# Attention and a split-precision feed-forward layer in one kernel: the low part of the inner layer given to ScalarE and GpSimd beside the last attention units, and room made for their keys

## The chip, the core and the metric

The kernel runs on one core of one Trainium2 chip. The metric is the device time of one execution in microseconds (us). Five engines work side by side, each through its own queue in order: TensorE (PE; PEld is its weight load), VectorE (DVE), ScalarE (ACT), GpSimd (POOL) and SyncE (SP), which issues most transfers.

## What is computed

```python
# q_l, k_l, v_l: 8 batches x 8 heads x 512 x 64;  q_g, k_g, v_g: 8 x 8 x 32 x 64
k_all, v_all = concat(k_g, k_l), concat(v_g, v_l)
out_g = softmax(q_g @ k_all.T / 8) @ v_all            # 32 global queries see all 544 keys
s_l   = concat(q_l @ k_g.T / 8, where(|i-j| <= 32, q_l @ k_l.T / 8, -1e9))
out_l = softmax(s_l) @ concat(v_g, v_l)               # 512 local queries: a band and the globals
x  = concat(out_g, out_l) as (8, 576, 512)
xn = (x - mean) / sqrt(var + 1e-6) * g_ln             # over the last axis
out = x + relu(xn @ w_ch1) @ w_ch2                    # 512 -> 2048 -> 512
```

## The kernel before

**Units and chunks.** Attention is done in units. 64 local units (a batch, a pair of heads, a half of 256 queries) come first; then 8 global units, each of four batches and a pair of heads (128 rows, 544 keys). Rows that are done make chunks for the feed-forward layer: chunks 0 to 7 of 512 local rows, and chunk 8 of the 256 global rows. While TensorE runs the layer for one chunk, the attention of the next is fitted in between.

**The layer** (class `Ffn`). A product in float32 quality is made of three products of high and low parts. For each of 16 inner blocks f, `first` makes 12 matmuls of 512 columns (line 836) into the bank `ph`; ScalarE writes the high part `hh` = relu(ph) (line 845); VectorE writes the low part `hl` = max(ph, 0) - hh (line 849). `second(f-1, t)`, four groups of 3 matmuls (line 861), takes `hh` and `hl` of the block before. So TensorE's order is first(f), second(f-1), first(f+1), second(f), and there is one `ph` for chunks of 512 rows.

**Visits.** At a visit TensorE computes the scores of one global unit (lines 667 and 678) and, right behind them, the weighted sums of the unit before (line 745). Between two visits VectorE takes row minima from the scores (`lowest`, line 690), ScalarE the exponentials (line 701), and the weights are turned: by VectorE in 16 or 32 transposes of 32x128 (line 729) into `gpt`, and partly by TensorE (`turn`, line 715) with a ScalarE copy (line 719), as `BY_DVE` says for each unit. The last 32 keys' weights go by four transposes (`turn_last`, line 736) onto the diagonal of a zeroed tile `lasts`, and meet a stacked tail of the values, `gvt` (64 KB).

**Transfers.** A unit's queries (`gq`, 128 KB, two buffers), keys (`gk`, 1152 KB, one buffer) and values (`tmp`, 1024 KB in two transfers, and `gvt`) are loaded by SyncE's queue. After a visit that scores unit n come n's values, then the queries and keys of n+1. The tiles of the global units lie in the pool `apool1`, which takes the place of the local units' pool `apool0` (u_e, u_v, p, pt).

**Order.** Each engine's queue is written out ahead by a planner (`Plan.emit`). Every operation has an engine, a cost, a key and what it must follow; of what can start soonest, the smallest key goes first. The table `ORDER` fixes each queue up to the middle of chunk 5; from there the costs decide. For the transfers the planner reckons 0.9 per loading step of a global unit, sizes of 1.2 (keys) and 1.15 (values) MB at `WIRE` = 0.42 MB per us, and a visit's cost as

```python
cost = 0.42 + 0.55 * len(us) + 1.12 * len(prev) + (0.1 if us and prev else 0)
```

`LATENCY` is 0.2 and `LANDING` 0.5. Chunk 7 may hold visits from the places `GLOBAL` = (0, 4, 8, 11, 14, 17, 20, 24) on, in half blocks of the layer; a visit whose inputs the planner sees later comes later. The chip itself waits for the real data, by semaphores.

Of the kernel before, what the change touches and what calls it, by code (L numbers as in the profile page):

```python
# [54 lines left out]
LAST_SUMS = 17  # L55
SOONER = 6.0
SECOND = 20.0
FIRST = 22
BEHIND = 2.1
GAP = 2.2  # L60
# [19 lines left out]
APPLY_ACT = (1,)  # L80
IN_FLIGHT = 8
STORING = 6.0
BY_DVE = (4, 4, 4, 0, 0, 0, 0, 0)

ORDER = {
    "PE": """
# [220 lines left out]
class Operation:  # L307
    def __init__(self, engine, cost, key, run, after, behind, late, size):
        self.engine, self.cost, self.key, self.run = engine, cost, key, run
        self.after = flat(after)  # L310
        self.behind, self.late, self.size, self.end = behind, late, size, None

    def lands(self):
        return self.end + self.late + LATENCY

    def ready(self):
        t = self.behind.end if self.behind else 0.0
        for a in self.after:
            same = a.engine == self.engine and not a.size
            t = max(t, a.end if same else a.end + a.late + LATENCY)  # L320
        return t

@with_exitstack
def attention_ffn_kernel(
# [1 line left out]
    tc: tile.TileContext,  # L326
    eq: bass.AP,
    ev: bass.AP,
    gq: bass.AP,
    gk: bass.AP,  # L330
    gv: bass.AP,
    gt: bass.AP,
# [6 lines left out]
    NQ, NV = eq.shape[4], ev.shape[4]  # L339
    D = P // 2  # L340
    SG = WIN
    SA = gk.shape[4] - SG
    S = SA - SG
    DM = HP * P
    KT = DM // P
# [15 lines left out]
    def f32(ap):  # L361
        return ap.bitcast(F32)
# [153 lines left out]
    class Local:  # L516
# [7 lines left out]
        def load(self, part):  # L524

            if self.alone:
                if part != 1:
                    shape, tag = [P, 2 * (KT * P + DM)], UNITS[units.index(self)]
                    u = wpool.tile(shape, F32, name="u", tag=tag)
                    self.parts = u[:, :NQ], u[:, NQ:NQ + NV]  # L530
            elif part == 0:
                self.parts = self.ap.tile([P, NQ], F32, name="u_e", bufs=2), None
            else:
                self.parts = self.parts[0], self.ap.tile([P, NV], F32, name="u_v", bufs=2)
            self.e, v = self.parts
            if v is not None:
                self.v = v.rearrange("p (w d) -> p w d", w=8)
            dma(self.parts[part], (eq, ev)[part][self.at])

        def score(self, sc):  # L540
            self.mn = small.tile([P, 4], F32, name="mn", bufs=4)
            self.sm = small.tile([P, 4], F32, name="sm", bufs=4)
            self.p = self.ap.tile([P, 4, P], F32, name="p", bufs=3)
            self.sc = sc
            for qb in range(2):
                for g in range(4):
                    gp = slice(g * WIN, (g + 1) * WIN)
                    w = 4 * qb + g
                    k0 = 8 + w + w // 3
                    for h in range(2):  # L550
                        hd = slice(h * D, (h + 1) * D)
                        nc.tensor.matmul(  # L552
                            sc[h][gp, qb * P:(qb + 1) * P],
                            self.e[hd, w * WIN:(w + 1) * WIN],
                            self.e[hd, k0 * WIN:(k0 + 4) * WIN],
                            start=True,
                            stop=True,
                            tile_position=(h * D, g * WIN),
                            skip_group_check=True,
                        )  # L560
# [77 lines left out]
    class Global:  # L638
# [4 lines left out]
        def load(self, part):  # L643
            ap = self.ap
            if part == 0:
                self.q = ap.tile([P, BG, 2 * SG], F32, name="gq", bufs=2)
                self.k = ap.tile([P, BG, SA + SG], F32, name="gk")
                dma(self.q, gq[self.at])
                dma(self.k, gk[self.at])
            else:  # L650
                self.v = [wtmp.tile([P, 2, 4, P], F32, name="tmp", bufs=2) for _ in range(BG // 2)]
                self.t = ap.tile([P, P], F32, name="gvt")
                for k, v in enumerate(self.v):
                    dma(v, gv[self.at][:, 2 * k:2 * k + 2])
                dma(self.t, gt[self.at])
# [75 lines left out]
        def turn_last(self):  # L731


            for i in range(BG):
                ip = slice(i * SG, (i + 1) * SG)
                nc.vector.transpose(out=lasts[0][ip, :, ip], in_=self.p[ip, :, 512:SA])

        def sums(self, pv):
            self.pv = pv
            for h in range(2):  # L740
                hd = slice(h * D, (h + 1) * D)
                for c in range(5):
                    for i in range(BG):
                        ip = slice(i * SG, (i + 1) * SG)
                        nc.tensor.matmul(  # L745
                            pv[ip, hd],
                            self.pt[:, h, c, ip] if c < 4 else lasts[0][:, h, ip],
                            self.v[i // 2][:, i % 2, c, hd] if c < 4 else self.t[:, hd],
                            start=c == 0,
                            stop=c == 4,  # L750
                            tile_position=(0, i * SG),
                            skip_group_check=True,
                        )
# [66 lines left out]
    class Ffn:  # L820
# [20 lines left out]
        def high(self, f):  # L841
# [2 lines left out]
            self.hq[f] = hh, hl  # L844
            nc.scalar.activation(hh[:, :self.n], self.ph[f][:, :self.n], AF.Relu)  # L845

        def low(self, f):
            hh, hl = self.hq[f]
            nc.vector.scalar_tensor_tensor(  # L849
                hl[:, :self.n], self.ph[f][:, :self.n], 0.0, f32(hh[:, :self.n]),  # L850
                ALU.max, ALU.subtract,
            )
# [55 lines left out]
    pools = []  # L908

    def begin(phase):  # L910
        if pools:
            pools.pop().__exit__(None, None, None)
        if phase == 2:
            wcm.__exit__(None, None, None)
            return
        cm, ap = open_pool(f"apool{phase}")
        pools.append(cm)
        for u in phases[phase]:
            u.ap = ap
        if phase == 1:  # L920
            last = ap.tile([P, 2, P], F32, name="lasts")
            nc.gpsimd.memset(last, 0.0)
            lasts.append(last)

    lasts = []

    def into(u):

# [7 lines left out]
    def begin_plan(plan):  # L936
# [229 lines left out]
        def visit(key, us, prev, nxt):  # L1166
# [31 lines left out]
            for j, u in enumerate(us):  # L1198
                exps = []
                before = []  # L1200
                if locals_:
                    for k in range(4):
                        before.append(op("DVE", 0.21, key + 0.1, lambda u=u, k=k: u.lowest(k), v,
                                         before[-1:], late=0.1))
                        exps.append(op("ACT", 0.39, key + 0.2, lambda u=u, k=k: u.exp(k), before[-1],
                                       late=0.1))
                        banks[k // 2].append(before[-1])
                else:
                    for h in range(2):
                        for part in range(2):  # L1210
                            before.append(op("DVE", (0.65, 0.15)[part], key + 0.1,
                                             lambda u=u, h=h, part=part: u.lowest(h, part), v,
                                             before[-1:], late=0.1))
                            banks[2 if part else h].append(before[-1])
                        exps.append(op("ACT", 0.75, key + 0.2, lambda u=u, h=h: u.exp(h), before[-1],
                                       late=0.2))
                t = op("POOL", 0.23, key + 0.3, lambda u=u: u.total(), exps)
                inverse_of[u] = op("DVE", 0.17, key + 1.0, lambda u=u: u.inverse(), t)
                if not locals_:
                    u.parts = n = BY_DVE[phases[1].index(u)]  # L1220
                    rr, o = [], []
                    for k in range(32 if n else 16):
                        o.append(
                            op("DVE", 0.31 if k < 16 else 0.06 + 0.25 * n / 4, key + (2 if k < 16 else SECOND),
                               lambda u=u, k=k: u.transposes(k // 16, k // 4 % 4, k % 4),
                               exps[k // 16], o[-1:])
                        )
                    last = op("DVE", 0.5, key + 2, lambda u=u: u.turn_last(), exps, o[0])
                    if n < 4:
                        t = op("PE", 0.1 + 0.45 * (4 - n) / 4, key + 1.0, lambda u=u: u.turn(att(1, "tp")), use(1, rr),  # L1230
                               exps[1], late=0.3)
# [87 lines left out]
        pe = [None]  # L1319
        turns_free = flat(list(low.values()))  # L1320
        hh, hl, second, adds, outs = {}, {}, {}, {}, {}
        xts = {0: (xt, (xh, xl))}

        def chain(*args, **kw):
# [3 lines left out]
        for c, chunk in enumerate(chunks):  # L1328
# [29 lines left out]
            for f in range(NF + 1):  # L1358
                key = nominal(c, f)
                if f < NF:  # L1360
                    for i, k in enumerate((2, 1, 0)):
# [5 lines left out]
                        waits = []  # L1367
                        if i == 0:
                            if not wide:
                                waits = [hl.get((c, f - 2)), hl[c - 1, NF - 1] if f == 0 else None,  # L1370
                                         use(0, []) if f == 1 else None]
                            else:
                                waits = [hl.get((c, f - 1)) if f else hl.get((c - 1, NF - 1))]
                            if c == f == 0:
                                waits += lowest[n0 - 2] + lowest[n0 - 1]
                        if f == 1 and i == 0 and 0 in beside:
# [10 lines left out]
                    if 2 * f in beside:  # L1387
                        beside[2 * f].behind = end
                    hh[c, f] = op("ACT", 0.59 if wide else 0.38, key - URGENT, lambda f=f, box=box: box[0].high(f),
                                  end, second.get((c, f - 2, nt - 1)))  # L1390
                    hl[c, f] = op("DVE", 0.66 if wide else 0.39, key - URGENT, lambda f=f, box=box: box[0].low(f),
                                  hh[c, f])
                if f:
                    for t in range(nt):
                        waits = []
# [179 lines left out]
```

## Time and profile before

| | |
|---|---|
| median of 3 runs | 903.01 us (901.91 to 903.97) |
| profiled execution | 904.45 us |
| its span, first to last instruction | 902.3 us |
| TensorE busy | 886.8 us (98%) |
| VectorE busy | 724.1 us (80%) |
| ScalarE busy | 309.7 us (34%) |
| GpSimd busy | 40.7 us (5%) |
| moved by transfers | 119.87 MB |

An engine's busy time is a share of the whole span, and matmuls overlap, so "busy" for TensorE means that it has no gap, not that each matmul runs at its shortest. The idle time ahead of an instruction names what ended it.

### The profile page before, as it was taken

The page shows a single profiled execution, that of the slowest core. Times are in us where ns is not written, and L with a number is a line of the kernel's source. Part 1 is how long each engine was busy: PE and PEld are TensorE (multiplying, and loading weights), DVE is VectorE, ACT ScalarE, POOL GpSimd, SP SyncE. Part 2 cuts the span into 40 slices and gives each one's busy share as a digit, 9 for nine tenths or more (in the row PEclk, how much of TensorE's full clock was granted, in tenths as well). Part 3 has the DMA queues.
Part 4 walks back from the last instruction along what each step waited for, and adds up shares of the span by engine and source line. Part 5 has one row for each costly group of instructions (what it writes and reads, how often), then busy time and mean ns, then how long its engine had stood idle before and what let it go on. Part 6 is the DMA issues. An engine that isn't in the chain of part 4 may idle for free.

```text
span 902.3 us, 21499 instructions
## 1 busy us (share of the span) xinstructions
PE 886.8 (98%) x8493; PEld 704.9 (78%) x8493; DVE 724.1 (80%) x2544; ACT 309.7 (34%) x878; POOL 40.7 (5%) x133
## 2 busy tenths in 40 slices
PE   7899999999999999999999999999999999999998
PEld 4588787777787787878788787778778777777897
DVE  5899999789878888788878897888879998866611
ACT  7798873232224222322323222322323222222211
POOL 4100100000000000000000000000000000000000
PEclk9899999999999999999999999999999999999999
DMA  9697736324034313324332403332331524455400
GB/s 347 246 330 219 282 110 208 103 79 149 34 111 140 117 52 126 102 78 149 107 100 99 149 2 123 106 119 103 125 102 48 187 94 151 174 183 178 138 22 23
DMA packets 44021, 119.87 MB, mean 133 GB/s; under 512 B 5265, under 2 KB 7313, under 8 KB 42897
## 3 DMA queue, kind: packets, MB, share of 16 engines
q1 hardware_dynamic: 43728, 118.25, 38.0%
q8 instruction: 66, 1.08, 0.5%
q14 instruction: 35, 0.28, 0.1%
q10 hardware_dynamic: 192, 0.26, 0.1%
HBM read 100.67 MB, written 17.83 MB: 131 GB/s over the span
## 4 chain that ended last, share of the span: by engine, by line
PE 81%; DVE 2%; DMA 2%; SPq 0%; issue 0%
PE ph L836 37%; PE acc L861 37%; PE sc L552 3%; PE pv L607 3%; DMA gk<-in_gk 2%; PE pv L745 1%; PE sc L667 1%; DVE pt L599 1%; DVE xl L814 0%; DVE ob L873 0%; DVE w L466 0%; SPq L411 0%; DVE hl L849 0%; PE tp L715 0%; DVE tmp L456 0%
## 5 line engine op out<-in xcount | busy, mean ns | idle before, releaser
L861 PE MATMUL acc<-w,hh 128*128 128x512 f32 x1088 | 342.1, 395 | 0.0
L836 PE MATMUL ph<-xh,w 128*128 128x512 f32 (+1 forms) x1216 | 307.9, 379 | 0.8 <-DVE hl L849 0.6
L836 PEld LDWEIGHTS ph<-xh,w 128*128 128x128 f32 x1216 | 215.5, 188 | 49.0 <-DVE hl L849 1.1
L861 PEld LDWEIGHTS acc<-w,hh 128*128 128x128 f32 x1088 | 204.8, 188 | 47.9
L845 ACT ACTIVATE hh<-ph 128x512 fp32r<-128x512 f32 (+1 forms) x144 | 82.9, 576 | 440.1 <-PE ph L836 410.5
L861 PE MATMUL acc<-w,hl 128*128 128x512 f32 x544 | 217.9, 401 | 0.0
L599 DVE STREAM_TRANSPOSE pt<-p 32x128 f32<-32x128 f32 x768 | 207.2, 289 | 8.5
L849 DVE SCALAR_TENSOR_TENSOR hl<-ph,hh 128x512 fp32r<-128x512 f32 (+1 forms) x144 | 95.3, 662 | 101.4 <-ACT hh L845 100.4
L836 PE MATMUL ph<-xl,w 128*128 128x512 f32 x512 | 141.2, 397 | 0.0
L576 ACT ACTIVATE p<-p,mn 128x128 f32<-128x128 f32 x256 | 99.7, 392 | 93.3 <-DVE mn L564 93.2
L804 DVE STREAM_TRANSPOSE tmp<-x 32x128 f32<-32x128 f32 x384 | 116.1, 302 | 5.8
L861 PEld LDWEIGHTS acc<-w,hl 128*128 128x128 f32 x544 | 102.1, 188 | 23.8
L836 PEld LDWEIGHTS ph<-xl,w 128*128 128x128 f32 x512 | 95.6, 188 | 23.7 <-DVE xl L814 0.2
L564 DVE CUSTOM_DVE_ANT_0 p<-sc,mask 128x128 f32<-128x128 f32 x256 | 60.9, 285 | 21.7 <-PE sc L552 21.2
L729 DVE STREAM_TRANSPOSE gpt<-gp 32x128 f32<-32x128 f32 x176 | 53.3, 303 | 2.9
L576 ACT ACTIVATION_READ_ACCUMULATOR p<-p,mn 128x1 f32 x256 | 48.2, 188 | 0.0
L619 POOL TENSOR_SCALAR ri<-sm 128x4 f32<-128x4 f32 x64 | 16.9, 264 | 640.3 <-ACT p L576 638.6
L626 DVE TENSOR_TENSOR x<-pv,ri 128x256 f32<-128x256 f32 x64 | 24.8, 418 | 11.1 <-PE pv L607 11.1
L552 PEld LDWEIGHTS sc<-u_e 64*32 64x32 f32 x1792 | 24.9, 105 | 10.2 <-issue 8.8
L552 PE MATMUL sc<-u_e 64*32 64x128 f32 x1792 | 32.4, 274 | 0.0
L607 PE MATMUL pv<-u_v,pt 128*32 128x64 f32 x1792 | 30.8, 220 | 0.0
L607 PEld LDWEIGHTS pv<-u_v,pt 128*32 128x32 f32 x1792 | 26.3, 110 | 5.7 <-issue 5.7
(71 smaller groups left out, 493.4 us busy)
## 6 DMA issues: line engine op xcount, KB each, us to landing
u_v<-in_ev SPq DMA_DIRECT2D x56, 512.0 KB, 4.8
u_e<-in_eq SPq DMA_DIRECT2D x56, 336.0 KB, 5.9
raw<-in_wd SPq DMA_DIRECT2D x32, 512.0 KB, 7.1
gk<-in_gk SPq DMA_DIRECT2D x8, 1152.0 KB, 7.6
xs<-x SPq DMA_DIRECT2D x32, 256.0 KB, 6.3
ob<-xs SPq DMA_DIRECT2D x32, 256.0 KB, 5.3
out<-ob SPq DMA_DIRECT2D x32, 256.0 KB, 3.4
tmp<-in_gv SPq DMA_DIRECT2D x16, 512.0 KB, 4.7
```

The costliest lines, as they stand in the source:

```text
L552: nc.tensor.matmul(sc[h][gp, qb * P:(qb + 1) * P], self.e[hd, w * WIN:(w + 1) * WIN], self.e[hd, k0 * WIN:(k0 + 4) * WIN], start=True, sto ...
L564: nc.vector.tensor_tensor_reduce(out=self.p[:, c], in0=self.sc[h][:, qb * P:(qb + 1) * P], in1=masks[self.at[2], qb], scale=-QSCALE, scala ...
L576: nc.scalar.activation(self.p[:, c], self.p[:, c], AF.Exp, bias=self.mn[:, c:c + 1], scale=-1.0, accum_out=self.sm[:, c:c + 1],)
L599: nc.vector.transpose(out=self.pt[rp, :, gp], in_=self.p[gp, :, rp])
L607: nc.tensor.matmul(pv[gp, qb * P + h * D:qb * P + h * D + D], self.pt[:, 2 * h + qb, gp], self.v[:, 4 * qb + g, h * D:(h + 1) * D], start= ...
L626: nc.vector.tensor_tensor(self.x[:, :, hp * P:(hp + 1) * P].rearrange("p q (h d) -> p q h d", h=2), self.pv[:, :256].rearrange("p (q h d) ...
L729: nc.vector.transpose(out=self.pt[rp, h, :n, ip], in_=p[ip, :, r])
L804: nc.vector.transpose(out=dst[rp, 2 * half:2 * half + 2, :, i], in_=src[ip, :, k:k + 2, r])
L836: nc.tensor.matmul(self.ph[f][:, :self.n], w[:, kt, :], xx[kt][:, :self.n], start=begins and kt == 0, stop=ends and kt == KT - 1,)
L845: nc.scalar.activation(hh[:, :self.n], self.ph[f][:, :self.n], AF.Relu)
L849: nc.vector.scalar_tensor_tensor(hl[:, :self.n], self.ph[f][:, :self.n], 0.0, f32(hh[:, :self.n]), ALU.max, ALU.subtract,)
L861: nc.tensor.matmul(self.acc[t], a[:, ts], w, start=(f == 0 and i == 0), stop=(f == NF - 1 and i == 2),)
```

## The change

Four things are changed. From block 11 of chunk 6 to block 14 of chunk 7, except each chunk's last block, the low part is made in two steps: ScalarE writes relu(ph) a second time as plain float32 (`hw`), and GpSimd subtracts `hh` from it (`low_pool`); `ph` is free after ScalarE's second write. Units 3 and 4 are turned wholly by VectorE (`BY_DVE`). Queries and keys of a unit come in one transfer into one tile, in a pool of its own (`bp`) that takes the place of the local units' u_e and p; all else is in `ap`. The last keys' weights are turned by one transpose of all 128 rows into a tile `gl`, and the tail of the values has zeros in the other batches' rows instead (256 KB). Besides, some costs in the planner are altered: VectorE's transposes and minima are a little dearer, the last keys' cheaper, and the minima may follow a visit's scores 1.2 sooner (`SUMS`) where sums stand behind the scores.

```diff
+SUMS = 1.2
+LOW_ON_POOL = {6: 22, 7: 0}
-BY_DVE = (4, 4, 4, 0, 0, 0, 0, 0)
+BY_DVE = (4, 4, 4, 4, 4, 0, 0, 0)
...
-            t = max(t, a.end if same else a.end + a.late + LATENCY)
+            t = max(t, a.end if same else a.end + a.late + LATENCY - (SUMS if a is self.scored else 0.0))
...
-                self.parts = self.ap.tile([P, NQ], F32, name="u_e", bufs=2), None
+                self.parts = self.bp.tile([P, NQ], F32, name="u_e", bufs=2), None
...
-            self.p = self.ap.tile([P, 4, P], F32, name="p", bufs=3)
+            self.p = self.bp.tile([P, 4, P], F32, name="p", bufs=3)
...
-                self.q = ap.tile([P, BG, 2 * SG], F32, name="gq", bufs=2)
-                self.k = ap.tile([P, BG, SA + SG], F32, name="gk")
-                dma(self.q, gq[self.at])
-                dma(self.k, gk[self.at])
+                both = self.bp.tile([P, BG, 2 * SG + SA + SG], F32, name="gk")
+                self.q, self.k = both[:, :, :2 * SG], both[:, :, 2 * SG:]
+                dma(both, gk[self.at])
...
-                self.t = ap.tile([P, P], F32, name="gvt")
+                self.t = ap.tile([P, BG, P], F32, name="gvt")
...
-            for i in range(BG):
-                ip = slice(i * SG, (i + 1) * SG)
-                nc.vector.transpose(out=lasts[0][ip, :, ip], in_=self.p[ip, :, 512:SA])
+            self.last = self.ap.tile([P, 2, SG], F32, name="gl")
+            nc.vector.transpose(out=self.last, in_=self.p[:, :, 512:SA])
...
-                            self.pt[:, h, c, ip] if c < 4 else lasts[0][:, h, ip],
-                            self.v[i // 2][:, i % 2, c, hd] if c < 4 else self.t[:, hd],
+                            self.pt[:, h, c, ip] if c < 4 else self.last[:, h],
+                            self.v[i // 2][:, i % 2, c, hd] if c < 4 else self.t[:, i, hd],
...
+        def wide(self, f, ap):
+            self.hw = ap.tile([P, 512], F32, name="hw")
+            nc.scalar.activation(self.hw[:, :self.n], self.ph[f][:, :self.n], AF.Relu)
+
+        def low_pool(self, f):
+            hh, hl = self.hq[f]
+            nc.gpsimd.tensor_tensor(
+                hl[:, :self.n], self.hw[:, :self.n], f32(hh[:, :self.n]), op=ALU.subtract
+            )
...
-        if phase == 1:
-            last = ap.tile([P, 2, P], F32, name="lasts")
-            nc.gpsimd.memset(last, 0.0)
-            lasts.append(last)
+        for at in ("bp", "ap"):
+            cm, pool = open_pool(f"{at}{phase}")
+            pools.append(cm)
+            for u in phases[phase]:
+                setattr(u, at, pool)
...
-                            before.append(op("DVE", (0.65, 0.15)[part], key + 0.1,
+                            before.append(op("DVE", (0.75, 0.25)[part], key + 0.1,
                                              lambda u=u, h=h, part=part: u.lowest(h, part), v,
                                              before[-1:], late=0.1))
+                            if prev:
+                                before[-1].scored = v
...
-                            op("DVE", 0.31 if k < 16 else 0.06 + 0.25 * n / 4, key + (2 if k < 16 else SECOND),
+                            op("DVE", 0.316 if k < 16 else 0.06 + 0.256 * n / 4, key + (2 if k < 16 else SECOND),
...
-                    last = op("DVE", 0.5, key + 2, lambda u=u: u.turn_last(), exps, o[0])
+                    last = op("DVE", 0.2, key + 2, lambda u=u: u.turn_last(), exps, o[0])
...
-                    hl[c, f] = op("DVE", 0.66 if wide else 0.39, key - URGENT, lambda f=f, box=box: box[0].low(f),
-                                  hh[c, f])
+                    if 2 * f >= LOW_ON_POOL.get(c, 99) and f < NF - 1:
+                        copied = op("ACT", 0.59, key - URGENT,
+                                    lambda f=f, box=box: box[0].wide(f, phases[1][0].ap), hh[c, f],
+                                    [hl[k] for k in hl if k in on_pool][-1:])
+                        on_pool.add((c, f))
+                        read[c, f] = copied
+                        hl[c, f] = op("POOL", 1.3, key - URGENT, lambda f=f, box=box: box[0].low_pool(f), copied)
+                    else:
+                        hl[c, f] = op("DVE", 0.66 if wide else 0.39, key - URGENT, lambda f=f, box=box: box[0].low(f),
+                                      hh[c, f])
+                        read[c, f] = hl[c, f]
```

The first product of the next block then waits for `read` (the last reader of `ph`) where it waited for `hl`.

## Rows read from the trace of the kernel before

**Rows 1.** The page: span, and each engine's busy time, share and instructions.

```profile
span 902.3 us, 21499 instructions
...
PE 886.8 (98%) x8493; PEld 704.9 (78%) x8493; DVE 724.1 (80%) x2544; ACT 309.7 (34%) x878; POOL 40.7 (5%) x133
```

**Rows 2.** Busy time by stretch (chunk 5, chunk 7), granted clock, transfers.

```profile
545.36:644.29 98.93, 98.93 (x897) 79.16 (x897) 83.14 (x308) 27.81 (x90) 3.26 (x10) 1.00 0.30 104
...
744.51:843.12 98.61, 97.79 (x1110) 76.17 (x1109) 74.83 (x258) 23.59 (x48) 2.09 (x8) 1.00 0.51 174
```

**Rows 3.** TensorE in order of time: start, length, and idle time before.

```profile
709.87 1.09 PE L667 MATMUL sc<-gk,gq 64*32 64x512 f32 x16 [0.70 <-DMA gk<-in_gk]
...
760.04 1.09 PE L667 MATMUL sc<-gk,gq 64*32 64x512 f32 x16
...
778.05 1.09 PE L667 MATMUL sc<-gk,gq 64*32 64x512 f32 x16
...
791.20 1.09 PE L667 MATMUL sc<-gk,gq 64*32 64x512 f32 x16 [0.74 <-DMA gk<-in_gk]
...
804.51 1.09 PE L667 MATMUL sc<-gk,gq 64*32 64x512 f32 x16
...
816.65 1.09 PE L667 MATMUL sc<-gk,gq 64*32 64x512 f32 x16
...
829.43 1.09 PE L667 MATMUL sc<-gk,gq 64*32 64x512 f32 x16
```

**Rows 4.** The chain that ended last, in order of time: start, length, what.

```profile
703.48 6.34 DMA gk<-in_gk
...
753.10 2.81 PE acc L861 x12
755.92 2.80 PE ph L836 x12
...
782.72 8.34 DMA gk<-in_gk
...
798.54 0.44 PE tp L715 x4
...
829.35 0.08 issue
```

**Rows 5.** Groups by line: count, busy time, mean ns, idle time before.

```profile
L849 DVE SCALAR_TENSOR_TENSOR hl<-ph,hh 128x512 fp32r<-128x512 f32 (+1 forms) x144 | 95.3, 662 | 101.4 <-ACT hh L845 100.4
L845 ACT ACTIVATE hh<-ph 128x512 fp32r<-128x512 f32 (+1 forms) x144 | 82.9, 576 | 440.1 <-PE ph L836 410.5 <-DVE pt L599 29.7
...
L729 DVE STREAM_TRANSPOSE gpt<-gp 32x128 f32<-32x128 f32 x176 | 53.3, 303 | 2.9
...
L736 DVE STREAM_TRANSPOSE lasts<-gp 32x64 f32<-32x64 f32 x32 | 7.6, 236 | 0.4
...
L378 POOL TENSOR_SCALAR_AFFINE_SELECT band<-band 128x192 f32<-128x192 f32 x2 | 0.7, 348 | 0.1
```

**Rows 6.** VectorE in order of time: last local transposes, one unit's last keys.

```profile
698.37 3.19 DVE L599 STREAM_TRANSPOSE pt<-p 32x128 f32<-32x128 f32 x10
...
809.54 0.99 DVE L736 STREAM_TRANSPOSE lasts<-gp 32x64 f32<-32x64 f32 x4
```

**Rows 7.** SyncE's queue in order of time: issues of two units' keys.

```profile
809.72 0.42 SPq L411 DMA_DIRECT2D gk<-in_gk  x1
...
821.97 0.42 SPq L411 DMA_DIRECT2D gk<-in_gk  x1
```

**Rows 8.** These two transfers: KB, us from issue to landing.

```profile
gk<-in_gk SPq DMA_DIRECT2D x1, 1152.0 KB, 6.0
...
gk<-in_gk SPq DMA_DIRECT2D x1, 1152.0 KB, 7.3
```

**Rows 9.** From first values' issue to keys' landing: last three columns clock, transfers' share, GB/s.

```profile
806.89:815.70 8.81, 8.81 (x48) 7.14 (x41) 8.16 (x31) 2.87 (x6) 0.22 (x1) 1.00 0.76 277
...
819.03:829.30 10.27, 10.27 (x53) 8.02 (x45) 7.98 (x29) 2.87 (x6) 0.22 (x1) 1.00 0.73 238
```

More of the change, by code (lines that the diff above doesn't have):

```diff
@@ L311, in __init__ @@
         self.behind, self.late, self.size, self.end = behind, late, size, None
+        self.scored = None
     def lands(self):
@@ L328, in attention_ffn_kernel @@
     ev: bass.AP,
-    gq: bass.AP,
     gk: bass.AP,
@@ L341, in attention_ffn_kernel @@
     SG = WIN
-    SA = gk.shape[4] - SG
+    SA = gk.shape[4] - 3 * SG
     S = SA - SG
@@ L910, in begin @@
     def begin(phase):
-        if pools:
+        while pools:
             pools.pop().__exit__(None, None, None)
@@ L915, in begin @@
             return
[L916 to L919, printed above, removed]
-        if phase == 1:
-            last = ap.tile([P, 2, P], F32, name="lasts")
-            nc.gpsimd.memset(last, 0.0)
-            lasts.append(last)
-    lasts = []
+        for at in ("bp", "ap"):
[3 more added lines that the diff above has]
+                setattr(u, at, pool)
     def into(u):
@@ L1321, in begin_plan @@
         hh, hl, second, adds, outs = {}, {}, {}, {}, {}
+        read, on_pool = {}, set()
         xts = {0: (xt, (xh, xl))}
@@ L1369, in begin_plan @@
                             if not wide:
-                                waits = [hl.get((c, f - 2)), hl[c - 1, NF - 1] if f == 0 else None,
+                                waits = [read.get((c, f - 2)), read[c - 1, NF - 1] if f == 0 else None,
                                          use(0, []) if f == 1 else None]
                             else:
-                                waits = [hl.get((c, f - 1)) if f else hl.get((c - 1, NF - 1))]
+                                waits = [read.get((c, f - 1)) if f else read.get((c - 1, NF - 1))]
                             if c == f == 0:
@@ L1553 @@
     ).view(np.int64)
+    tails = np.zeros((bg, hp, 4, sg, 4, 2 * d), dtype=v4.dtype)
+    for i in range(4):
+        tails[:, :, i, :, i] = v4[..., s:s + sg, :][:, i]
     arrays = {
@@ L1556 @@
         "in_ev": ve.reshape(b, hp, 2, 128, -1),
-        "in_gq": beside(by_four(tr(q_g)), sg),
-        "in_gk": beside(by_four(kc), sg),
+        "in_gk": np.concatenate([beside(by_four(tr(q_g)), sg), beside(by_four(kc), sg)], axis=4),
         "in_gv": v4[..., :s, :].reshape(bg, 4, hp, 4, 128, 2 * d).transpose(0, 2, 4, 1, 3, 5),
-        "in_gt": v4[..., s:s + sg, :].transpose(0, 2, 1, 3, 4).reshape(bg, hp, 4 * sg, 2 * d),
+        "in_gt": tails.reshape(bg, hp, 4 * sg, 4, 2 * d),
         "in_g": moe_g_ln.reshape(-1, 128).T,
```

## The prediction, made before the change was run

> **What bounds the kernel now.** I read the engines' shares of the span first: TensorE 886.8 of 902.3 us, VectorE 724.1, GpSimd 40.7 [rows 1]. Next came the stretches, one per chunk of the inner layer. Chunk 5 (545 to 644 us) has TensorE busy for all of its 98.93 us; chunk 7, where most global units stand (744.51 to 843.12), 97.79 of 98.61 us [rows 2]. So this core runs at TensorE's instructions end to end, and a change is worth only two things: instructions taken from TensorE, and gaps in its row. The reader should see that VectorE, at 80% of the span, is not the bound, though the change works almost wholly on VectorE. What VectorE does is to say when the next visit (scores of unit n and weighted sums of unit n-1) can start.
>
> TensorE's order in time gives the visits and the gaps [rows 3]. Two visits show a wait: 0.70 us at 709.87 and 0.74 us at 791.20, both for the keys (gk). The chain of waits shows the same at 791 and 0.08 us of idle time at 829.35 [rows 4]. That is 1.52 us, and it is all that can be won by removing waits; the granted clock is 1.00 in both chunks [rows 2], so nothing is to be had there.
>
> **What the change takes away.** (1) Units 3 and 4 are no longer turned on TensorE. One such turn costs 0.44 us of the chain [rows 4]; two are 0.88 us. Their 16 further VectorE transposes each cost 16 x 0.303 = 4.8 us of VectorE [rows 5], hidden as long as the visit behind them is not late.
>
> (2) Keys' room. The first keys went out at 703.48, after the last local sums, and their visit waited 0.70 us [rows 3, 4]. In the new pools they lie only over the tiles u_e and p, whose last reader is VectorE's last transpose of the local units. That ends at 698.37 + 3.19 = 701.56 [rows 6]. So they go out 1.9 us sooner. They carry 1280 instead of 1152 KB in one transfer (the queries used to go ahead); at the 277 GB/s of a loaded stretch [rows 9] 128 KB are 0.5 us. They land near 703.48 + 6.34 - 1.9 + 0.5 = 708.4, and TensorE comes to them at 709.17. The wait of 0.70 us goes; at worst (not sooner at all) it stays.
>
> (3) The low part of 19 inner blocks (4 in chunk 6, 15 in chunk 7) leaves VectorE: 0.66 us each [rows 5]. ScalarE gets a second write of 0.58 us, priced by its first [rows 5], and GpSimd a subtraction of 128x512, of which no row shows one. From below: GpSimd's select over 128x192, a smaller operation with one input, takes 0.348 us [rows 5], so 0.35 us is a floor. From above: if all of that time grows with the elements, 512/192 x 0.348 = 0.93 us, and twice that for two inputs 1.86 us. I take 1.2 us, between the ends and nearer the upper, since the second input is certain. The result is wanted only when the next block's first product is through: 2.81 + 2.80 us after the block's own [rows 4]. Less 0.6 us for each of ScalarE's writes, 4.4 us are left for GpSimd. Either bound fits, so this costs nothing while ScalarE is not stuck; it is 24% busy in that chunk [rows 2]. The hidden-layer bank is free after ScalarE's two writes, 1.2 us, where the next block comes 2.8 us later. If that cover goes, the cost is the excess, block by block.
>
> [...]
>
> (4) The last keys' weights: one operation instead of four. Four take 0.99 us [rows 6], one 0.24 [rows 5], so 0.75 us of VectorE per unit. Its price is the widened tail of the values: 256 instead of 64 KB per unit.
>
> **What it adds: an order that runs ahead of the transfers.** The planner starts a visit when, by its own costs, keys, values and VectorE's transposes are ready. At present VectorE is last in most of them: visits stand 18.0 us apart where VectorE turns a unit (760.04 to 778.05) and 12.1 and 12.8 apart where TensorE helps (804.51, 816.65, 829.43) [rows 3]. The change cuts VectorE's part. For a unit that TensorE helps with, in the planner's costs: scores usable 1.49 us after the visit's start (before 2.69), the first exponentials at 3.94, sixteen transposes 5.06, last keys and reciprocal 0.37, hand-over 0.2: 9.6 us. By its costs for the transfers the keys are there after 2.19 (visit) + 0.5 + 0.9 + 1.15/0.42 + 1.2/0.42 + 0.7 = 9.9 us. It puts the visit at the next boundary of a TensorE operation of 0.7 or 0.93 us, so 9.9 to 10.8 after the one before, and the real visit is some 0.3 us longer than its 2.19: I take 10.7 us. These costs decide the order only; what follows is priced by rows.
>
> The keys don't come that fast. From the start of a visit to the landing of the next keys: 804.51 to 809.72 + 6.0 = 815.7, that is 11.2 us; 816.65 to 821.97 + 7.3 = 829.3, 12.6 us [rows 3, 7, 8]; 778.05 to 791.06, 13.0 us [rows 3, 4]. They are issued behind the values, and these wait for the sums of the visit. The change puts 192 KB more ahead of them, 0.7 us at 277 and 0.8 us at 238 GB/s [rows 9], and drops one issue of 0.43 us: 0.3 to 0.4 later. For the two visits whose unit before is turned partly by TensorE and which need keys (scores of units 6 and 7) I take (11.2 + 12.6)/2 + 0.4 = 12.3 us against 10.7: a wait of 1.6 us each. Bounds: 11.2 + 0.3 - 10.9 = 0.6 and 13.0 + 0.4 - 10.2 = 3.2 us. While TensorE waits there, the whole inner layer behind it in its queue waits too, and with it ScalarE's and GpSimd's parts; nothing later makes it up, since TensorE is full to the end. The visits before them (units turned wholly by VectorE, now up to unit 4) have 3.94 + 32 transposes of 0.316 + about 0.6 = 14.6 us or more between them, longer than any landing: no wait, and the 0.74 us at 791 goes, as unit 3 is now one of them. The last visit needs no keys.
>
> **Sum.** -0.70 - 0.74 - 0.08 - 0.88 + 2 x 1.6 = +0.8 us. The profiled execution took 904.45 us (span 902.3), so 905.25 by its measure; the median of the runs shown, 903.01, lies 1.44 below it, so 903.8.
>
> **Rivals.** *Full gain.* The transfers keep up, or the visits stand at 12 us as now: ScalarE, with two writes of 0.6 us per block ahead of the exponentials, holds VectorE's transposes back by up to 1.2 us, and the keys have landed within 11.2 us once. For it: today's 12.1 and 12.8 us show 0 and 0.08 us of waiting [rows 3, 4]. Then -2.4 us: 900.6.
>
> *GpSimd holds VectorE off* (slower). The place is VectorE's transposes between the visits that score units 1 to 5. If each of the 2.6 subtractions in 14.6 us stopped VectorE for 1.2 us, VectorE would be 3.1 us late. The sums begin only 1.1 us into a visit, and the planner's exponentials are some 0.5 us too long, so 1.6 us are forgiven; the rest, 1.5 us, in four visits, is 6.0 us, and the whole is +6.8: 909.8. It decides from 0.6 us of blocking each. Against it: GpSimd has 40.7 us of work in the span [rows 1], too little for the trace to show either way. [...]
>
> *The keys' room does nothing*: the first keys still go out after 703.48, because something else in that queue is late. Then the 0.70 us stays: +1.5, 904.5.
>
> **How the numbers follow.** About 0.2%, 1.8 us, is what a measurement of this kernel can tell. The forecast case gets 0.50; its own range, with waits of 0.6 to 3.2 us in each of two visits, is -1.2 to +4.0 us, 901.8 to 907.0. Of its half, 0.03 is faster by over 0.2%, 0.34 within, 0.13 slower. Full gain has 0.33 (0.30 faster, 0.03 within, as 2.4 is near the bound), the keys' room 0.06 (within), GpSimd 0.07 and anything else that makes TensorE wait 0.04 (slower). Together: faster 0.33, within 0.43, slower 0.24. The range runs from 900.3, just under the full gain, to 906.4; it leaves out GpSimd's case and the forecast's upper edge.
>
> **What the profile will show.** TensorE's row: no wait at the first keys' visit; two turns fewer (12 instead of 20 matmuls at the turn's line); the visits of units 6 and 7 some 12 us after the ones before, each with a wait for the keys of over 1 us. The visits before them 14.5 to 16 us apart, without one. GpSimd's subtraction at 0.9 to 1.9 us, VectorE's transposes still 0.30 us. The prediction is wrong if TensorE waits nowhere in 740 to 843 us, if transposes grow longer beside GpSimd, or if the inner layer's second product waits for its low part.

## The result and the profile after

The changed kernel took 910.97 us (median of 4, 910.07 to 913.47) against 903.49 us (median of 4 as well): a ratio of 1.0079 with a 95% interval of 1.0061 to 1.0098, slower by 0.8%. The forecast was 903.8 us, 900.3 to 906.4. The profiled execution, 913.47 us, is the slowest of the four, so its waits may lie at the long end.

The page's head, to be held against [rows 1]:

```profile
span 911.7 us, 21513 instructions
...
PE 890.9 (98%) x8485; PEld 706.9 (78%) x8485; DVE 715.0 (78%) x2533; ACT 317.9 (35%) x895; POOL 64.7 (7%) x151
```

VectorE has 9 us less to do, GpSimd 24 us more, and the span is 9.4 us longer. TensorE is "busy" for 4 us more with eight matmuls fewer: something runs slower. Chunk 7 in stretches, as in [rows 2] (clock, transfers' share and GB/s stand last):

```profile
744.70:786.54 41.84, 41.84 (x381) 32.81 (x382) 34.06 (x124) 11.44 (x24) 8.36 (x9) 1.00 0.54 192
786.54:803.50 16.96, 16.61 (x173) 12.58 (x172) 13.63 (x50) 5.65 (x11) 3.37 (x4) 1.00 0.48 172
803.50:821.94 18.44, 14.59 (x191) 10.13 (x195) 7.74 (x30) 4.30 (x9) 4.07 (x4) 0.91 0.42 143
821.94:839.10 17.16, 15.18 (x230) 11.96 (x230) 7.76 (x29) 3.36 (x7) 1.50 (x2) 0.80 0.45 155
```

The first 42 us have no gap. The loss lies between 803 and 839 us, and there the granted clock falls too. TensorE's visits in order of time, as in [rows 3]:

```profile
709.49 1.09 PE L668 MATMUL sc<-gk 64*32 64x512 f32 x16
...
757.91 1.09 PE L668 MATMUL sc<-gk 64*32 64x512 f32 x16
...
773.36 1.09 PE L668 MATMUL sc<-gk 64*32 64x512 f32 x16
...
788.56 1.09 PE L668 MATMUL sc<-gk 64*32 64x512 f32 x16
...
803.50 1.20 PE L836 MATMUL ph<-xh,w 128*128 128x512 f32 x4 [0.35 <-ACT hw L849]
...
805.56 1.09 PE L668 MATMUL sc<-gk 64*32 64x512 f32 x16
...
819.77 1.96 PE L668 MATMUL sc<-gk 64*32 64x512 f32 x16 [3.85 <-DMA gk<-in_gk]
...
835.20 1.41 PE L668 MATMUL sc<-gk 64*32 64x512 f32 x16 [1.98 <-DMA gk<-in_gk]
```

The first keys' wait is gone. The visits after units turned by VectorE stand 15.2 to 17.0 us apart, with no wait. The two behind partly turned units wait for their keys, and the same 16 score matmuls last 1.96 us instead of 1.09. The chain, as in [rows 4]:

```profile
810.70 9.03 DMA gk<-in_gk
...
819.77 1.96 PE sc L668 x16
821.73 0.21 PE pv L679 x15
821.94 2.33 PE pv L745 x80
...
826.14 9.02 DMA gk<-in_gk
```

The clock around the first of these waits, from the same view as the stretches above:

```profile
816.00:818.00 2.00, 0.00 (x0) 0.00 (x0) 0.00 (x0) 0.35 (x1) 1.26 (x1) 1.00 0.77 327
818.00:819.77 1.77, 0.00 (x0) 0.00 (x1) 0.00 (x0) 0.00 (x0) 0.00 (x0) 0.72 0.10 41
819.77:821.94 2.17, 2.17 (x36) 0.84 (x40) 0.12 (x1) 0.00 (x0) 0.00 (x0) 0.50 0.00 0
821.94:824.20 2.26, 2.26 (x81) 2.09 (x81) 0.58 (x2) 0.00 (x0) 0.00 (x0) 0.50 0.04 7
824.20:826.20 2.00, 2.00 (x10) 1.62 (x7) 1.87 (x10) 1.47 (x3) 0.00 (x0) 0.65 0.51 135
```

TensorE stood idle from 815.9 us, the granted clock fell to half (0.50 from 819.00 us on) before the keys were there, and the visit and the first of the next products ran at it. At the second wait it fell only when the visit had begun: 0.73 from 835.20 to 836.61 us, then 0.50 to its end.

Two visits of 2.4 us took 1.96 + 0.21 + 2.33 = 4.5 and (835.20 to 839.10) 3.9 us, and the products behind the first 0.8 us more: 2.1 + 1.5 + 0.8 = 4.4 us lost to the clock. With the waits of 3.85, 1.98 and 0.35 us that is 10.6 us lost. The old waits of 1.52 us and two turns of 0.88 us went: +8.2 us. A further 0.6 us lies in the visit at 741.7 us, whose sums met their values late, and 0.4 us ahead of chunk 6, in the start: 9.2 of the span's +9.4 us.

What TensorE waits for in the end is a small rest of the load. From 817.50 us to the landing at 819.73 the 16 transfer engines are busy for 0.14 of the time, and for 0.10 through the whole of the second wait (833.22 to 835.16); in the kernel before, such a rest is some 1.0 us long (0.03 from 814.70 to 815.70). Why it is longer here, no run shows.

The groups by line, as in [rows 5]:

```profile
L730 DVE STREAM_TRANSPOSE gpt<-gp 32x128 f32<-32x128 f32 x208 | 63.0, 303 | 3.5
...
L853 POOL TENSOR_TENSOR hl<-hw,hh 128x512 fp32r<-128x512 f32 x19 | 24.4, 1286 | 82.5 <-ACT hw L849 82.5
...
L849 ACT ACTIVATE hw<-ph 128x512 f32<-128x512 f32 x19 | 11.2, 592 | 0.0
...
L736 DVE STREAM_TRANSPOSE gl<-gp 128x64 f32<-128x64 f32 x8 | 2.0, 245 | 0.1
```

GpSimd's subtraction takes 1.286 us, and VectorE's transposes 303 ns as before (each of the 208 between 290 and 310 ns).

### The profile page after: what moved, and what is told of

Its sections match the earlier page's. It is cut to its first block, busy times and chain, and to the rows that moved or that the text cites. A ratio compares the mean times of both kernels' runs of the same rounds, so it can differ in the third digit from the quotient of the medians.

```text
span 911.7 us, 21513 instructions
## 1 busy us (share of the span) xinstructions
PE 890.9 (98%) x8485; PEld 706.9 (78%) x8485; DVE 715.0 (78%) x2533; ACT 317.9 (35%) x895; POOL 64.7 (7%) x151
## 3 DMA queue, kind: packets, MB, share of 16 engines
q8 instruction: 66, 1.08, 0.5%
## 4 chain that ended last, share of the span: by engine, by line
PE 79%; DMA 3%; DVE 2%; SPq 1%; issue 0%; ACT 0%; ACTq 0%
PE ph L836 36%; PE acc L871 36%; PE sc L554 3%; PE pv L609 3%; DMA gk<-in_gk 2%; PE pv L745 1%; PE sc L668 1%; DMA xs<-x 1%; DVE pt L601 1%; SPq L413 1%; DVE xl L814 0%; DVE ob L883 0%; DVE w L468 0%; DVE hl L859 0%; DVE tmp L458 0%
## 5 line engine op out<-in xcount | busy, mean ns | idle before, releaser
L859 DVE SCALAR_TENSOR_TENSOR hl<-ph,hh 128x512 fp32r<-128x512 f32 (+1 forms) x125 | 82.1, 657 | 96.3 <-ACT hh L845 95.6
L730 DVE STREAM_TRANSPOSE gpt<-gp 32x128 f32<-32x128 f32 x208 | 63.0, 303 | 3.5
L628 DVE TENSOR_TENSOR x<-pv,ri 128x256 f32<-128x256 f32 x64 | 24.8, 418 | 11.3 <-PE pv L609 11.3
L554 PEld LDWEIGHTS sc<-u_e 64*32 64x32 f32 x1792 | 24.9, 105 | 10.2 <-issue 8.8
L691 DVE TENSOR_SCALAR_CACHE_REDUCE gp<-sc 128x512 f32<-128x512 f32 x16 | 11.0, 689 | 25.7 <-PE sc L668 25.1
```

The costliest lines, as they stand in the source:

```text
L554: nc.tensor.matmul(sc[h][gp, qb * P:(qb + 1) * P], self.e[hd, w * WIN:(w + 1) * WIN], self.e[hd, k0 * WIN:(k0 + 4) * WIN], start=True, sto ...
L628: nc.vector.tensor_tensor(self.x[:, :, hp * P:(hp + 1) * P].rearrange("p q (h d) -> p q h d", h=2), self.pv[:, :256].rearrange("p (q h d) ...
L730: nc.vector.transpose(out=self.pt[rp, h, :n, ip], in_=p[ip, :, r])
L859: nc.vector.scalar_tensor_tensor(hl[:, :self.n], self.ph[f][:, :self.n], 0.0, f32(hh[:, :self.n]), ALU.max, ALU.subtract,)
```

## The experiments

Theory one: the planner's order runs ahead of the transfers, at the visits that score units 6 and 7. Theory two: GpSimd's subtraction or ScalarE's second write costs the time. Theory three: the wider tail or the joined transfer makes the keys late. Each edit is made on the changed kernel unless said otherwise; ratios are to the kernel before on the same chip, with a 95% interval.

**A planner that knows how long the loads take.**

```diff
-            u.size = 1.2, 1.15
+            u.size = 2.05, 2.15
```

> The changed kernel with nothing altered but two sizes in the planner: keys 2.05 and values 2.15 MB instead of 1.2 and 1.15, so that by its reckoning the next keys land 14.3 us after a visit starts (9.9 before), as the trace of the changed kernel shows them land (14.2 us after the visit at 805.56). Theory one (the order runs ahead of the transfers: visits of units 6 and 7 wait 3.85 and 1.98 us, and the granted clock falls to 0.50 behind each wait): the waits and the clock's loss go, about 10 us, so 900.5 to 902.5 us. Theory two (GpSimd's subtraction or ScalarE's second write costs the time): nothing of it changes here, 908 to 912 us. Theory three (the wider tail of the values and the joined transfer slow the keys down): the keys land as late as before, but TensorE has other work meanwhile; it gives the same as theory one.

904.92 us, ratio 1.0018 (1.0005 to 1.0030): 6 us less than the change with not one instruction altered but the order, and all 19 subtractions in place. No visit waits. Theory two could not give that. It missed the 900.5 to 902.5 us, because the last visit now comes too late (its sums at 845.2 us, at 841.8 before the change): the last rows' turn for chunk 8 waits, and the clock falls to 0.53 behind it. TensorE in order of time, then a stretch:

```profile
849.33 0.27 PE L796 MATMUL t<-ident,x 128*128 128x128 f32 x1
850.90 0.77 PE L796 MATMUL t<-ident,x 128*128 128x128 f32 x5 [1.30 <-ACT x L499]
852.32 0.44 PE L796 MATMUL t<-ident,x 128*128 128x128 f32 x2 [0.65 <-DVE xh L814]
```

```profile
852.50:854.50 2.00, 2.00 (x10) 1.79 (x10) 1.03 (x3) 0.47 (x1) 0.00 (x0) 0.53 0.04 10
```

**The low part back on VectorE.**

```diff
-LOW_ON_POOL = {6: 22, 7: 0}
+LOW_ON_POOL = {}
```

> The changed kernel with the low part left on VectorE in all blocks; the rest of the change stays. Theory one: VectorE's part between tight visits grows by one or two low parts of 0.66 us, the planner's visits of units 6 and 7 stand about 11.7 us after the ones before instead of 10.4, the keys still land after 13 to 14 us: two waits of 1.5 to 3 us, some of the clock's loss, 905 to 909 us. Theory two: with the subtraction gone the loss is gone, 901 to 903.5 us. Theory three: as theory one.

907.36 us, 1.0055 (1.0034 to 1.0077): 3.6 us less than the change at the median, though the intervals overlap. Without GpSimd and the second write the two waits are still there, and the visits begin 13.0 and 14.3 us after the ones before:

```profile
808.23 1.09 PE L668 MATMUL sc<-gk 64*32 64x512 f32 x16
...
821.23 1.09 PE L668 MATMUL sc<-gk 64*32 64x512 f32 x16 [1.95 <-DMA gk<-in_gk]
...
835.53 1.09 PE L668 MATMUL sc<-gk 64*32 64x512 f32 x16 [3.25 <-DMA gk<-in_gk]
```

In this execution the clock stayed at 1.00 through a wait of 3.25 us and the visit behind it; in the changed kernel it fell behind waits of 3.85 and 1.98 us. So a wait's price is not its length alone.

**The narrow tail again** (64 KB, four transposes onto the zeroed diagonal).

```diff
-                self.t = ap.tile([P, BG, P], F32, name="gvt")
+                self.t = ap.tile([P, P], F32, name="gvt")
...
-            self.last = self.ap.tile([P, 2, SG], F32, name="gl")
-            nc.vector.transpose(out=self.last, in_=self.p[:, :, 512:SA])
+            for i in range(BG):
+                ip = slice(i * SG, (i + 1) * SG)
+                nc.vector.transpose(out=lasts[0][ip, :, ip], in_=self.p[ip, :, 512:SA])
```

> The changed kernel with the old tail of the values: 64 KB in one stacked tile, the last keys' weights by four transposes onto a zeroed diagonal. Theory one: 192 KB less ahead of the keys is 0.7 us per visit, VectorE's three more transposes are 0.75 us, so the two waits shrink by 0.7 to 1.5 us each, and the clock falls as before or for a shorter time: 906 to 910 us. Theory three: the keys land 11 to 13 us after a visit's start again, the waits all but go: 902 to 904 us. Theory two: 910 to 911 us.

905.95 us, 1.0026 (1.0007 to 1.0045), 5 us less than the change, just under what theory one gave and above theory three. The waits are 1.47 and 1.26 us, without a fall of the clock, and the keys land 11.8 and 12.1 us after the visit before:

```profile
803.99 1.09 PE L668 MATMUL sc<-gk 64*32 64x512 f32 x16
...
815.82 1.09 PE L668 MATMUL sc<-gk 64*32 64x512 f32 x16 [1.47 <-DMA gk<-in_gk]
...
827.92 1.09 PE L668 MATMUL sc<-gk 64*32 64x512 f32 x16 [1.26 <-DMA gk<-in_gk]
```

So with the narrow tail the kernel is faster, and two waits remain. How much of that is the 192 KB isn't shown: in the last experiment below the keys land as early with the wide tail.

**The wait filled with work**, to price the clock.

```diff
+                if us and us[0] in phases[1][6:]:
+                    a = ident.bitcast(BF16)
+                    for _ in range(12):
+                        nc.tensor.matmul(
+                            sc[0], a[:, :P], a.unsqueeze(1).to_broadcast([P, 2, 2 * P]), start=True, stop=True,
+                        )
```

> The changed kernel with 12 more matmuls of 512 bf16 columns (some 2.6 us, written into the score bank and overwritten) ahead of the scores of units 6 and 7, to measure what the clock's fall costs by itself. The keys land no sooner. Theory one with the clock as a second part: TensorE does useless work while it waits, the granted clock stays at 1.00, and the visits take 2.4 us instead of 4.4 and 3.9: 4 us less, but the second wait grows by up to 1.3 us as the visit before it is no longer slow: 906 to 908.5 us. If the clock's fall costs nothing by itself: 910 to 912 us.

907.76 us, 1.0056 (1.0036 to 1.0075): 3.2 us less at the median with 5.5 us of useless matmuls in it (2.77 and 2.76 us for the two fills, each reckoned at some 2.6), though the intervals overlap. In this execution TensorE also waits 1.64 us for the inner bank (`ph`) at 802.72 us and 0.65 us for keys. The clock stays at 1.00 and the visit behind the first fill takes 2.4 us:

```profile
815.00:817.70 2.70, 2.70 (x16) 1.09 (x16) 0.00 (x0) 0.56 (x2) 1.27 (x1) 1.00 0.53 224
817.70:820.10 2.40, 2.40 (x114) 1.71 (x113) 0.70 (x2) 0.00 (x0) 0.00 (x0) 1.00 0.00 0
```

One execution would not show that the fill did this, as the clock also held through unfilled waits above. Over whole executions the mean granted clock is 0.994 to 1.000 in the eight of this run and 0.988 to 0.992 in the four of the changed kernel.

**Keys issued before values.**

```diff
-                load_part(u, 0, key + 0.6, v)
+                load_part(u, 0, key + (0.6 if isinstance(u, Local) else 0.4), v)
```

The smaller key goes first; values have 0.5.

> The changed kernel with the loads behind a visit in the other order: the next unit's queries and keys are issued before this unit's values; the keys' buffer is free as soon as the scores are read, 1.2 us sooner than the values'. Planner's sizes as in the change, so visits of units 6 and 7 are again planned some 10.4 us after the ones before. Theory one: the keys land about 9 us after the visit's start, no score waits any more; but the values land 13 to 14 us after it, and the sums of the same visit want them 1.1 us after its start, so they wait 1.5 to 2.7 us each, mostly at the full clock: 904 to 907 us. If only the keys' place in the queue were the matter: 901 to 902 us.

901.49 us, 0.9981 (0.9967 to 0.9995): faster than both, and better than I expected of theory one. The visits stand 10.29 and 10.75 us apart, as the planner has them, without a wait, and the values are there too. Issues with KB and us to landing (the tail's issue is at 806.58 us, so it lands at 814.5), and the sums that use them:

```profile
gk<-in_gk SPq DMA_DIRECT2D x1, 1280.0 KB, 7.0
tmp<-in_gv SPq DMA_DIRECT2D x2, 512.0 KB, 7.5
gvt<-in_gt SPq DMA_DIRECT2D x1, 256.0 KB, 7.9
```

```profile
813.45 1.09 PE L668 MATMUL sc<-gk 64*32 64x512 f32 x16
814.33 0.33 PE L679 MATMUL pv<-gk 64*32 64x32 f32 x16
814.58 0.68 PE L745 MATMUL pv<-tmp,gpt 128*32 128x64 f32 x32
```

My expectation had the loads take as long as in the other order. They begin 1.4 us after the visit's start, with the scores read, instead of 2.4 with the sums done, and all had landed 11.3 us after it instead of 14.2. So 1.0 us of this is the earlier begin; why the same bytes then took 9.9 us instead of 11.8, no run shows.

**Six units on VectorE**, `BY_DVE = (4, 4, 4, 4, 4, 4, 0, 0)`.

> The changed kernel with unit 5 turned wholly by VectorE as well. Theory one: only one visit (unit 7's scores) is still planned 10.4 us after the one before, so one wait for keys of 2 to 4 us; a turn of 0.44 us less on TensorE; but VectorE spreads the visits, and the last one comes 3 to 4 us later against the chunk's end, as it did with the larger planner's sizes, where TensorE waited 2 us there: 904 to 909 us. If the transposes moved to VectorE are the cost themselves: over 911 us.

908.3 us, 1.0057 (1.0037 to 1.0076). One wait for keys (2.28 us) came as expected; the wait at the chunk's end did not, and one of 2.59 us for the inner bank, which is taken up below, came instead. That the time lies in the expected range is partly luck.

**Three units on VectorE**, `BY_DVE = (4, 4, 4, 0, 0, 0, 0, 0)`.

> The changed kernel with units 3 and 4 turned partly by TensorE again, as before the change: only the low part's move, the keys' room, the last keys' one operation and the planner's costs remain. Theory one: four visits (scores of units 4 to 7) are now planned some 10.4 to 11 us after the ones before, so four waits for keys of 1 to 4 us with the clock's fall behind the longer ones, and two turns of 0.44 us more: 911 to 920 us. The rival that the fifth unit's turning on VectorE costs the time: 903 us or less.

913.69 us, 1.0097 (1.0068 to 1.0125): four visits wait, as theory one has it, and turning the fifth unit on VectorE is no cause.

```profile
784.65 1.95 PE L668 MATMUL sc<-gk 64*32 64x512 f32 x16 [2.56 <-DMA gk<-in_gk]
...
798.55 1.09 PE L668 MATMUL sc<-gk 64*32 64x512 f32 x16 [0.82 <-DMA gk<-in_gk]
...
811.49 1.49 PE L668 MATMUL sc<-gk 64*32 64x512 f32 x16 [2.12 <-DMA gk<-in_gk]
...
825.91 1.96 PE L668 MATMUL sc<-gk 64*32 64x512 f32 x16 [2.56 <-DMA gk<-in_gk]
```

**Keys first, narrow tail, and sizes of 1.45 and 1.45** (three of the edits above together, the sizes smaller).

> A version meant to beat both: the changed kernel with the keys issued before the values, the old narrow tail of the values (with its four small transposes), and planner's sizes of 1.45 and 1.45 MB, by which keys and values are ready 11.2 us after a visit starts, so that the visits of units 6 and 7 stand some 11.9 us after the ones before. With the narrow tail the last transfer of a visit's loads landed 11.8 to 12.1 us after its start; keys first makes that the values', which are wanted 13 us after it. Theory one: no wait at a visit and the last visit some 3 us earlier than before against the chunk's end: the gain that was to be had, 900.5 to 902.5 us. A rival: GpSimd's or ScalarE's part costs 1 us or more: over 903 us.

900.38 us, 0.9968 (0.9951 to 0.9985), the lowest median of all, though the interval overlaps with that of keys first alone: no visit waits.

```profile
802.16 1.09 PE L668 MATMUL sc<-gk 64*32 64x512 f32 x16
...
813.85 1.09 PE L668 MATMUL sc<-gk 64*32 64x512 f32 x16
...
825.98 1.09 PE L668 MATMUL sc<-gk 64*32 64x512 f32 x16
```

**The kernel before with keys first.**

> The kernel before with one edit: a unit's keys are issued ahead of the values of the unit before it. Theory one: of its three waits for keys (0.70, 0.74 and 0.08 us) the two in chunk 7 go, the first, which waits for the local units' tiles, stays: 0.8 us less, 902.5 to 903 us. If the order of the loads were worth more than these waits, so that it and not the rest of the change makes the gain of 2 us that the changed kernel with keys first showed: 901 to 901.7 us.

902.9 us, 0.9997 (0.9988 to 1.0005): no difference that can be told. So the gain above is not the loads' order alone. The first keys' wait is the only one left, 0.92 us here, which the change's room removes.

**Keys first, low part on VectorE.**

> The changed kernel with keys first, and the low part left on VectorE in all blocks: what is the low part's move worth once no visit waits for keys? Theory one: visits behind a unit turned by VectorE stand 16.4 to 17.5 us apart instead of 15.4 to 16.7, the last visit comes 4 us later against the chunk's end and TensorE waits there for the last rows' turn, 0.5 to 2 us: 902 to 904 us, against 901.5 with the move. Theory two (the move itself costs time on ScalarE or GpSimd): under 901 us.

902.46 us, 0.9993 (0.9984 to 1.0001). The visits behind units turned by VectorE stand 16.4 to 17.9 us apart, and the last rows' turn waits 0.65 us. The move looks worth 1 us; the intervals overlap, so that is not settled.

**Queries and keys in two transfers again.**

```diff
-                both = self.bp.tile([P, BG, 2 * SG + SA + SG], F32, name="gk")
-                self.q, self.k = both[:, :, :2 * SG], both[:, :, 2 * SG:]
-                dma(both, gk[self.at])
+                self.q = self.bp.tile([P, BG, 2 * SG], F32, name="gq")
+                self.k = self.bp.tile([P, BG, SA + SG], F32, name="gk")
+                dma(self.q, gq[self.at])
+                dma(self.k, gk[self.at])
```

> The changed kernel with queries and keys in two transfers of 128 and 1152 KB again, into two tiles of the new pool; the order of the loads and the wide tail as in the change. If the joined transfer is what makes the keys land 14 to 15 us after a visit's start (theory three): they land 12 to 13 us after it, 904 to 907 us. Theory one (the planner's 10.4 us between the visits, and the bytes ahead of the keys): no better, one issue of 0.4 us more: 909 to 912 us.

910.48 us, 1.0080 (1.0051 to 1.0109): no gain in time. Its one profile (911.7 us) does not decide between the theories: the two waits for keys are 1.39 and 2.62 us, with the keys there 11.8 and 13.4 us after the visits before, sooner than in the changed kernel, and 2.96 us are lost to the inner bank. So whether the joining makes the keys late stays open; undoing it does not bring the time back.

**ScalarE's normalisation later in its queue.**

```diff
-                       late=STORING if isinstance(u, Local) else 0.0)
+                       late=STORING if isinstance(u, Local) else 9.0)
```

> The changed kernel with one cost in the planner altered: for global rows, ScalarE's normalisation is reckoned ready 9 us after its scale (it writes over rows that are being stored, and waited 5.8 us for these stores, with ScalarE's two writes of a block behind it). In four profiles with the changed order TensorE then waited 0.35, 1.64, 2.59 and 2.96 us for the inner bank. If that is a real part of the loss: no such wait, the two waits for keys as before, 908 to 910 us. If it is only a chance of single executions: 910.5 to 912 us. It may come too late for the last rows at the chunk's end, where the same operation stands on the way to the last chunk: then TensorE waits there instead, and the time is 911 us or more.

907.59 us, 1.0057 (1.0032 to 1.0083). The wait for the inner bank is gone, and here the keys' waits are shorter too (1.47 and 1.00 us, 11.8 us after the visits before, with the wide tail). The last rows' turn now waits 0.65 us. The expected 908 to 910 was just missed, and since the intervals of this run and of the change overlap, the share of this wait is not settled. The single executions run from 905.38 us, at a mean granted clock of 0.996, to 915.3 us at 0.986, so one profile is a weak witness for this order. What the wait for the inner bank is, ScalarE's row of the changed kernel shows: the normalisation of finished rows waits for their stores and the next block's two writes stand behind it. The normalisation waited 4.97 us in the kernel before and 5.5 us with keys first, too, where TensorE did not wait.

```profile
801.66 0.81 ACT L499 ACTIVATE x<-x,rs 128x512 f32<-128x512 f32 x1 [5.80 <-DMA xs<-x]
802.38 0.58 ACT L845 ACTIVATE hh<-ph 128x512 fp32r<-128x512 f32 x1
802.86 0.58 ACT L849 ACTIVATE hw<-ph 128x512 f32<-128x512 f32 x1
```

## Why the prediction was wrong

The mechanism was the one that the forecast rested on; its size was not. The step that failed is the term "2 x 1.6 us" for the late keys: the waits were too short in it, and the clock behind them was put at nothing. In its place stand 5.83 us of waits and 4.4 us lost to the half clock behind them, 10.2 us in this execution. Point by point:

- **TensorE is the bound, and only its gaps and instructions count:** right. The span's +9.4 us is found in TensorE's row.
- **Two turns, 0.88 us:** right. 12 matmuls are left at the turn's line.
- **Keys' room, 0.70 us:** right, narrowly. The first keys went out at 702.02 us and took 7.3 us, where 6.8 were reckoned; the visit stands at 709.49 without a wait.
- **The low part at no cost:** nearly. 1.286 us on GpSimd for 1.2 taken, 0.592 on ScalarE for 0.58, transposes unchanged at 303 ns: the rival that GpSimd holds VectorE off is refuted. That this rival's 909.8 us lie near the measured time is chance. The condition that I set, "while ScalarE is not stuck", was broken once: the normalisation above, 0.35 us here and up to 2.96 us in the experiments. With keys first the kernel without the move is no faster (902.46 against 901.49 us).
- **Visits 10.7 us apart in the planner's order:** right. TensorE was ready 10.36 us after the visit at 805.56 (819.77 less 3.85). The lower bound of the wait has a slip: it takes 10.9 us where 10.8 + 0.3 give 11.1, so 0.4 and not 0.6 us; nothing hung on it.
- **Keys 12.3 us after the visit's start:** too short; 14.2 and 15.4 us. The upper bound of 13.4 did not hold them. With the wide tail and the loads' order unchanged, the visits that waited for keys in the other runs came 11.8 to 14.4 us after the ones before, so one trace of before, with three values from 11.2 to 13.0, was a thin base. The tail's bytes, taken at 0.3 to 0.4 us, may cost more: with the narrow tail the kernel is 5 us faster, and the intervals are apart. But bytes alone do not make the 14.2: with the same 2560 KB in the same order the next scores began 11.8 us after the visit's sums here (807.97 to 819.77 us; 224 GB/s from 807.94 to 819.73) and 9.4 us after them in the last experiment (807.63 to 817.03). How much is the bytes and how much chance and the clock is open. The 15.4 us have a cause of their own: the slow visit held the values' issue back to 824.04, 4.3 us after its start instead of 2.4.
- **The clock:** not in the sum at all. In the profile before, TensorE's waits were under 0.75 us in these chunks and the clock did not move, so no row of them priced a longer one. The start of the same trace did: behind a wait of 1.91 us the granted clock is 0.50 from 27.42 to 31.00 us, and 32 matmuls that took 0.65 us shortly before take 1.08.

```profile
21.72 0.65 PE L607 MATMUL pv<-u,pt 128*32 128x64 f32 x32
...
27.42 0.64 PE L607 MATMUL pv<-u,pt 128*32 128x64 f32 x11 [1.91 <-issue]
...
29.04 1.08 PE L607 MATMUL pv<-u,pt 128*32 128x64 f32 x32
```

At half the clock 3.6 us of work lose 1.8 us; by that row two such waits would have added some 3.6 us to the sum, an estimate from this one trace.

- **The range** could not hold it: even the forecast case's own upper edge, 907.0 us with both waits at their bound, lay 4 us below. The gain side of the sum, 2.4 us, fits the version without waits: keys first takes 2.0 us less than the kernel before, and 3.2 us less with the narrow tail and larger sizes.

## What to carry to other kernels

Where an order is written out ahead from costs, relieving the engine that came last hands the timing to the next input, and the costs of that input are then what counts: check the planner's time for a load against the trace before making anything else faster. Where a load is what the order waits for, loads into a buffer that is free early go ahead of loads into one that is free late; in the kernel before, whose waits for keys in these chunks were short, the same edit changed nothing that could be told. And price a wait on TensorE with what follows it: the wait itself (5.83 us here), the instructions behind it where the granted clock falls (4.4 us lost at 0.50 here, nothing behind the 3.25 us of another execution), and whatever those instructions hold back in turn (the values' issue, 4.3 us after the visit's start instead of 2.4).

## What was not expected of the hardware

Behind waits of 3.85 and 1.98 us without a matmul the granted clock stood at half for some 3 to 6 us of work; in another execution it stayed full through 3.25 us. With 2.77 us of useless matmuls in such a wait it was full, and the visit behind ran at its usual 2.4 us. With the same 2560 KB of transfers in the same order, the next scores began 9.4 us after a visit's sums in one execution and 11.8 us in another, and in the slower case the last 2.2 us passed with the transfer engines busy for 0.14 of the time.
